# Output weights of a decode attention kernel: rows of 1 KB by head, in place of rows of 4 and 2 KB with selection matmuls

## The chip, the cores and the metric

The kernel runs on one core of a Trainium2 chip. The metric is the device time of one execution in microseconds. Three runs of the kernel before took 1382.37, 1382.78 and 1384.41 us; the median, 1382.78 us, is the time before.

## What is computed

Two attention blocks for one decoded token and four batches, each with its own query weights, caches and output weights; the outputs stand side by side. Block A has 32 query heads on 8 key heads and looks at the last 2048 positions; block B has 32 heads of its own and looks at all 8192. Everything is bfloat16, a head has 128 elements.

```python
# A: x (4,1,512), k/v cache (4,8,8192,128), W = 2048, rep = 4
q = (x @ wq) as (B, 32, 1, 128)
k, v = last W rows of the caches, each head repeated rep times
p = softmax(q k^T * 128 ** -0.5)
a = (p v) as (B, 1, 32 * 128) @ wo          # wo: (4096, 512)
# B: the same with k/v cache (4,32,8192,128), all rows, rep = 1
out = concatenate([a, b], axis=-1)
```

The caches that are read hold 570 MB, and each element is used for one or four query heads only, so nearly all of the work is to bring them in.

## The kernel before, in words

**Stages.** Stage A has 8 chunks, one for each key head with its four batches: 2 MB of keys and 2 MB of values. Stage B has 64 chunks, one for each pair of heads and each batch: 4 MB of keys and 4 MB of values. Chunk numbers run through: `NCA` = 8 is the first chunk of B, `NC` = 72 their number. A chunk is split into groups of 8 tiles of 128 x 128.

**One chunk.** PE transposes each key tile into PSUM (`tr`, `emit_T`), DVE or ACT copies a group to `kt` (L476, L474), PE multiplies it with the queries (`sc`, `emit_S`). DVE takes maxima (L539; in stage A first L523 and L525, which pick the scores of each partition's own batch), ACT takes the exponentials (`pba` in A, `pbb` in B). Two `ms` matmuls (`stats_gmax`, `stats_exp`) carry the maxima across partitions. Then PE multiplies the probabilities with the value tiles into `po` (`emit_pv`), `norm_sum` sums the rows with a matmul of ones and `norm_out` writes the normalised head outputs to `oT` (A: 4 heads x 4 batches) or `oz` (B: 2 heads x 4 batches, once in two chunks), with the 128 elements of a head on the partitions.

**Output weights.** The output product adds, for each head, a matmul of 128 x 4 with 128 x 512 to `fin`, in PSUM from the first chunk to the last (`emit_fin`). The weights come in per chunk of A (`wor`, 512 KB for 4 heads) and per head pair of B (`wos`, 256 KB). In the kernel before, partition p of `wor` takes the four consecutive rows 4p to 4p + 3 of the 512, so a row of the load is 4 KB long; partition p of `wos` takes rows 2p and 2p + 1, 2 KB. A partition then no longer holds element p of every head, but elements 4i + r (2i + r) of the head that its quarter (half) stands for. So the head outputs are permuted alike: `emit_sel` multiplies `oT` with four masks `sel4`, or `oz` with two masks `sel2`, into columns of `ms`, and DVE copies each quarter or half to `zA` or `zB` (L670). For the last pair it is turned about: `emit_wol` brings the weights back into head order with the masks `back2` (PE, four matmuls into `tr`) and copies them to `wol` (ACT and DVE, L682, L684), so that after the last `po` only `oz`, two `fin` matmuls, a copy and the output's DMA are left. POOL makes the masks at the start.

**Order.** Every engine has its program written out by hand: `sch.add` puts an instruction at the end of its engine's list, with the events that it waits for. `keys_part(c)` interleaves the transposes and scores of chunk c with pieces of earlier chunks at given groups: in A the maxima of chunk c - 1 at group 2 and its exponentials at 3, `emit_sel(c - 2)` at 4, `norm_sum(c - 1)` at 6 and `emit_fin(c - 2)` at 7; in B `emit_sel` at 8 and `emit_fin` at 10 of every second chunk. `values_part` has the value matmuls of the chunk before, and the last two groups of scores.

**Loads.** All large loads are issued by SP in one fixed order. In A it goes: keys of c + 1, values of c, `wor` of c, keys of c + 2, and so on. Keys wait until the buffer's earlier keys are transposed (L354), values until the earlier values are multiplied, `wor` of c until `fin` of c - 2 (L331). In B the order is keys, values, keys, values (L372), with one `wos` load ahead of every fourth keys (L338), which waits for the last `fin` that used it. The last keys come in two halves (L369, L370) and the last values in five pieces (L363).

Of the kernel before, what the change touches and what calls it, by code (L numbers as in the profile page):

```python
# [12 lines left out]
P = 128  # L13
# [6 lines left out]
NSM = 2  # L20
# [2 lines left out]
LASTV = (64, 32, 16, 8, 8)  # L23

TRM0, BC0, L0, Q0, XT0 = 0, 256, 288, 320, 448
Z0 = Q0


class _Record:
# [129 lines left out]
def bass_concat_heads__sliding_block_cached__mha_block_cached__decode_kernel(  # L159
# [45 lines left out]
    with ExitStack() as es:  # L205
        block = es.enter_context(nc.Block())

        def sb(name, shape, dt):
            return es.enter_context(nc.sbuf_tensor(name, shape, dt))
# [29 lines left out]
        oT = sb("oT", [P, NSM, 16], BF16)  # L239
        oz = sb("oz", [P, 8], BF16)  # L240
        outsb = sb("outsb", [36, DO], BF16)
        sel4 = sb("sel4", [P, 4, P], BF16)
        sel2 = sb("sel2", [P, 2, P], BF16)
        back2 = sb("back2", [P, 2, 2, P], BF16)
        zA = sb("zA", [P, 2, 16], BF16)
        zB = sb("zB", [P, 8], BF16)
        wol = sb("wol", [P, 2, DO], BF16)
        tr = ps("tr", [P, NTRB, TG * P], BF16)
        sc = ps("sc", [P, 2, 512], F32)
        po = ps("po", [P, 512], F32)  # L250
# [30 lines left out]
        sch.add("pool", lambda e: e.memset(pbt[1][:, :, :], 0.0), key=("c_pb", 1))  # L281

        for r in range(4):
            sch.add("pool", lambda e, r=r: e.affine_select(
                out=sel4[:, r, :], in_=onesb[:, :], pattern=[[0, 4], [-4, 32]], compare_op=ALU.is_equal,
                fill=0.0, base=-r, channel_multiplier=1), waits=["c_onesb"])
        for r in range(2):
            sch.add("pool", lambda e, r=r: e.affine_select(  # L290
                out=sel2[:, r, :], in_=onesb[:, :], pattern=[[0, 2], [-2, 64]], compare_op=ALU.is_equal,
                fill=0.0, base=-r, channel_multiplier=1))
            for u in range(2):
                sch.add("pool", lambda e, r=r, u=u: e.affine_select(
                    out=back2[:, u, r, :], in_=onesb[:, :], pattern=[[1, P]], compare_op=ALU.is_equal,
                    fill=0.0, base=P * u - r, channel_multiplier=-2), key="c_sel" if r == u == 1 else None)


        half_of = {}
        held = [[] for _ in range(NH)]  # L300
        HALF_A = {"k": (8, 9), "v": (4, 5)}
# [21 lines left out]
        def wo_slot(g):  # L323
            return g % 2 if g < NCA - 1 else 2

        def dma_wo(g):

            src = A_wo[g * 4 * P:(g + 1) * 4 * P, :].rearrange("(p r) n -> p (r n)", r=4)
            slot = wo_slot(g)
            dst = wor[:, slot, :]  # L330
            sch.add_dma("sp", lambda e: e.dma_start(dst, src), "d_wo%d" % slot,  # L331
                        waits=[("fin", g - 2)] if g >= 2 and slot < 2 else [], key=("wo", g))

        def dma_wos(hp):


            src = B_wo[2 * hp * P:2 * (hp + 1) * P, :].rearrange("(p r) n -> p (r n)", r=2)
            sch.add_dma("sp", lambda e: e.dma_start(wos[:, :, :].rearrange("p r n -> p (r n)"), src), "d_wos",  # L338
                        waits=[("fin", NCA + 4 * hp - 1)] if hp else [], key=("wos", hp))

        def dma_kv(kind, c):
# [302 lines left out]
        def norm_out(c):  # L644
            if 0 <= c < NCA:
                m = c % NSM
                o, i0, i1 = oT[:, m, :], po[:, m * 16:m * 16 + 16], rinv[:, m, :]
            else:

                o, i0 = oz[:, :].rearrange("p (x y) -> p x y", x=2), bcast(po[:, 0:4], [[0, 2], [1, 4]])  # L650
                i1 = rz[:, :].rearrange("p (x y) -> p x y", x=2)
            waits = [("rinv" if 0 <= c < NCA else "rz", c), ("pv", c)] + ([("sm", c - 2 if c != NCA + 1 else NONE)] if c >= 2 else [])
            sch.add("dve", lambda e: e.tensor_tensor(out=o, in0=i0, in1=i1, op=ALU.mult), waits=waits, key=("oT", c))
            po_read[:] = [("oT", c)]

        def emit_sel(c):

            if 0 <= c < NCA:
                sel, x, n, z, k = sel4, oT[:, c % NSM, :], 16, zA[:, c % 2, :], 4
                free = [("fin", c - 2)] if c >= 2 else []  # L660
            else:
                sel, x, n, z, k = sel2, oz[:, :], 8, zB[:, :], 2
                free = [("fin", c - 2 if c - 2 >= NCA else NONE)] if c != NONE else []
            for r in range(k):
                pe_mm(ms[:, Z0 + r * n:Z0 + (r + 1) * n], sel[:, r, :], x,
                      waits=[("oT", c)] + ms_read if r == 0 else [], key=("sm", c) if r == k - 1 else None)
            for h in range(k):
                pp = slice(h * P // k, (h + 1) * P // k)
                src = ms[pp, Z0:Z0 + k * n].rearrange("p (r b h) -> p h r b", r=k, b=NB)[:, h]
                sch.add("dve", lambda e, src=src, pp=pp: e.tensor_copy(z[pp, :].rearrange("p (r b) -> p r b", r=k), src),  # L670
                        waits=[("sm", c)] + free if h == 0 else [], key=("z", c) if h == k - 1 else None)
            ms_read[:] = [("z", c)]

        def emit_wol():

            for u in range(2):
                o = tr[:, u, :].bitcast(F32)
                for r in range(2):
                    pe_mm(o, back2[:, u, r, :], wos[:, r, :], start=r == 0, stop=r == 1,
                          waits=[("wos2", NC - 1)] if u == r == 0 else [], key=("back", u) if r else None)  # L680
                if u == 0:
                    sch.add("act", lambda e, o=o: e.activation(wol[:, 0, :], o, ACTF.Copy), waits=[("back", 0)], key=("wol", 0))  # L682
                else:
                    sch.add("dve", lambda e, o=o: e.tensor_copy(wol[:, 1, :], o), waits=[("back", 1)], key=("wol", 1))  # L684

        def emit_fin(c):
            ab = 0 if 0 <= c < NCA else 1
            p0 = 0 if ab == 1 else 32
            if c == NC - 1:
                ov = oz[:, :].rearrange("p (b u) -> p b u", u=2)  # L690
                ops = [(ov[:, :, u], wol[:, u, :]) for u in range(2)]
                waits = [("oT", c), ("wol", 0), ("wol", 1)]
            elif ab == 1:
                ops = [(zB[:, r * NB:(r + 1) * NB], wos[:, r, :]) for r in range(2)]
                waits = [("z", c), ("wos2", c)]
            else:
                w = wor[:, wo_slot(c), :].rearrange("p (r n) -> p r n", r=4)
                ops = [(zA[:, c % 2, r * NB:(r + 1) * NB], w[:, r, :]) for r in range(4)]
                waits = [("z", c), ("wo", c)]
            lastc = NC - 1 if ab == 1 else NCA - 1  # L700
            for i, (l, r) in enumerate(ops):
                pe_mm(fin[p0:p0 + NB, :], l, r, start=False, stop=i == len(ops) - 1 and c == lastc,
                      waits=waits if i == 0 else [], key=("fin", c) if i == len(ops) - 1 else None)
            if c == lastc:
                sch.add("dve", lambda e: e.tensor_copy(outsb[p0:p0 + NB, :], fin[p0:p0 + NB, :]), waits=[("fin", c)], key=("osb", ab))
                sch.add_dma("sp" if ab == 1 else "act",
                            lambda e: e.dma_start(out[:, 0, ab * DO:(ab + 1) * DO], outsb[p0:p0 + NB, :]),
                            "d_o%d" % ab, waits=[("osb", ab)], key=("out", ab))
# [6 lines left out]
        def keys_part(c):  # L715
# [3 lines left out]
            for g in range(ch["NG"]):  # L719
# [8 lines left out]
                if 1 <= c < NCA and g == 6:  # L728
                    norm_sum(c - 1)
                if 2 <= c < NCA and g == 4:  # L730
                    emit_sel(c - 2)
                if 2 <= c < NCA and g == 7:
                    emit_fin(c - 2)
                if c >= NCA and c % 2 == 0 and g == 6:
                    norm_sum(ahead(c, 1))
                if c >= NCA and c % 2 == 1 and g == 8:
                    emit_sel(ahead(c, 2))
                if c >= NCA and c % 2 == 1 and g == 10:
                    emit_fin(ahead(c, 2))

# [25 lines left out]

        def finish_A():
            stats_gmax(NCA - 1)
            emit_sel(NCA - 2)
            stats_exp(NCA - 1)  # L770
            emit_fin(NCA - 2)
            norm_sum(NCA - 1)
            for g in range(chunks[NCA - 1]["NG"]):
                emit_pv(NCA - 1, g)
            pv_done(NCA - 1)
            emit_sel(NCA - 1)
            emit_fin(NCA - 1)

        emit_xT()
# [2 lines left out]
        for c in range(NC):  # L782
            if c == NCA:
                sch.mark()
                finish_A()
            keys_part(c)
            if c == 0:
                emit_q(1)

                pe_mm(fin[0:36, :], pbt[0][:, 1, 0:36], pbt[0][:, 1, 0:DO], stop=False, waits=["c_sel"])  # L790
            values_part(None if c == 0 else NONE if c == NCA else c - 1, c)
        sch.mark()
        norm_sum(NC - 1)
        emit_wol()
        for g in range(chunks[NC - 1]["NG"]):
            emit_pv(NC - 1, g)
        pv_done(NC - 1)
# [60 lines left out]
```

## Time and profile before

| | |
|---|---|
| median of three runs | 1382.78 us |
| profiled execution: time / span | 1382.37 / 1380.6 us |
| PE, DVE, ACT, POOL busy | 85%, 48%, 32%, 1% of the span |
| DMA, main queue | 587.22 MB, 25208 packets, 99.4% of 16 engines' span |
| keys of B, 4 MB | 26.8 us from issue to landing |
| `wor`, 512 KB (8 loads) / `wos`, 256 KB (16 loads) | 6.0 / 20.4 us from issue to landing |
| L670 to `zA` (32) / to `zB` (64) | 168 / 164 ns each on DVE |

The span is one execution by the hardware profiler; the time adds what lies around it. Every load is cut into packets (one for each contiguous row, shared among 16 DMA engines), and the profile counts them and the share of time in which the engines had one. "L408" is a line of the kernel's file; all matmuls are recorded at L408 and all transposes at L406, so they are told apart by the tile that they write. "x24" is a count.

### The profile page before, as it was taken

To read this page: it belongs to the slowest core of one execution; us is meant where nothing else is said; L and a number is where in the kernel's file an instruction comes from. 1 tells how busy PE (TensorE), PEld (TensorE's weight loads), DVE (VectorE), ACT (ScalarE), POOL (GpSimd) and SP (SyncE) were. 2 spreads that over 40 slices of the span, in tenths; PEclk is the share of its full clock that TensorE was granted. 3 is DMA by queue.
4 is the path that set the end of the run, shared out by engine and by line. 5 is a ranking of instruction groups with operands and counts; after the bars stand their busy time and mean duration, and the time that the engine had idled before them with its cause. 6 is when DMAs were issued, how large, how long until landed. Compare 5 with 4: busy or idle time off the path is not lost.

```text
span 1380.6 us, 59798 instructions
## 1 busy us (share of the span) xinstructions
PE 1175.7 (85%) x27001; PEld 1131.6 (82%) x27001; DVE 656.8 (48%) x1434; ACT 436.7 (32%) x650; POOL 7.4 (1%) x28
## 2 busy tenths in 40 slices
PE   4887898888889888888898888888988898888988
PEld 4776898887888888888898888787987888888887
DVE  1665464444445444444454445444544444444444
ACT  1543233332233323322333223232332233223332
POOL 2000000000000000000000000000000000000000
PEclk9899999999999999999999999999999999999999
DMA  9999999999999999999999999999999999999998
GB/s 401 421 393 402 388 439 426 432 433 428 438 430 428 433 428 438 430 429 433 428 431 436 429 433 428 431 436 432 430 432 427 436 432 430 433 426 432 437 425 349
DMA packets 25254, 587.53 MB, mean 426 GB/s; under 512 B 2817, under 2 KB 2833, under 8 KB 6289
## 3 DMA queue, kind: packets, MB, share of 16 engines
q1 hardware_dynamic: 25208, 587.22, 99.4%
q8 instruction: 16, 0.26, 0.1%
q14 instruction: 6, 0.04, 0.0%
q10 hardware_dynamic: 24, 0.01, 0.0%
HBM read 587.21 MB, written 0.01 MB: 425 GB/s over the span
## 4 chain that ended last, share of the span: by engine, by line
DMA 60%; PE 35%; DVE 3%; issue 1%; ACT 1%; DVEq 0%; SPq 0%; ACTq 0%
DMA kv<-in_B_k_cache_dram 56%; PE tr L406 21%; PE sc L408 9%; PE po L408 3%; DMA kv<-in_B_v_cache_dram 2%; DMA kv<-in_B_wq_dram 2%; PE fin L408 2%; PE ms L408 1%; DVE sA L525 1%; DVE kt L476 0%; DVE zA L670 0%; DVE sA L523 0%; ACT pba L588 0%; DVE sA L581 0%; ACT eA L585 0%
## 5 line engine op out<-in xcount | busy, mean ns | idle before, releaser
L406 PE MATMUL tr<-identb,kv 128*128 128x128 bf16 x8704 | 697.2, 230 | 160.0 <-DMA kv<-in_B_k_cache_dram 156.9
L476 DVE COPY kt<-tr 128x1024 bf16<-128x1024 bf16 x736 | 502.5, 691 | 441.5 <-PE tr L406 436.8
L406 PEld LDWEIGHTS tr<-identb,kv 128*128 128x128 bf16 x8704 | 552.7, 104 | 182.0 <-DMA kv<-in_B_k_cache_dram 98.3
L474 ACT ACTIVATE kt<-tr 128x1024 bf16<-128x1024 bf16 x352 | 360.3, 1024 | 629.3 <-PE tr L406 629.3
L408 PE MATMUL sc<-qb,kt 128*128 128x64 bf16 x8704 | 448.9, 196 | 11.6 <-DVE kt L476 11.4
L408 PEld LDWEIGHTS sc<-qb,kt 128*128 128x128 bf16 x8704 | 370.1, 101 | 16.9 <-DVE kt L476 13.8
L408 PE MATMUL po<-pbb,kv 128*128 128x64 bf16 x8320 | 293.9, 192 | 6.3 <-issue 4.4
L408 PEld LDWEIGHTS po<-pbb,kv 128*128 128x128 bf16 x8320 | 267.1, 97 | 8.6 <-issue 4.6
L573 ACT ACTIVATE pbb<-sc,negb 64x128 bf16<-64x128 f32 x128 | 51.2, 400 | 294.9 <-DVE negb L563 294.1
L539 DVE TENSOR_REDUCE rm<-sc 64x1 f32<-64x128 f32 x128 | 36.9, 289 | 95.1 <-PE sc L408 94.2
L551 DVE TENSOR_REDUCE gm<-ms 1x2 f32<-1x128 f32 (+1 forms) x72 | 20.1, 279 | 44.8 <-PE ms L406 44.7
L563 DVE COPY negb<-ms 128x1 f32<-128x1 f32 (+1 forms) x72 | 11.4, 159 | 53.6 <-PE ms L408 53.6
L408 PE MATMUL ms<-identf,gx 1*128 1x1 f32 (+1 forms) x144 | 27.6, 259 | 0.8 <-DVE zA L670 0.8
L408 PEld LDWEIGHTS ms<-identf,gx 1*128 1x128 f32 (+1 forms) x144 | 21.5, 186 | 4.9 <-DVE zA L670 0.9
L573 ACT ACTIVATION_READ_ACCUMULATOR pbb<-sc,negb 64x1 f32 x128 | 23.7, 185 | 0.0
L406 PE MATMUL ms<-identf,rm 128*1 128x128 f32 (+1 forms) x72 | 19.6, 273 | 2.3 <-DVE rm L534 2.3
L408 PE MATMUL po<-pba,kv 128*128 128x64 bf16 x512 | 19.8, 198 | 0.5 <-ACT pba L588 0.5
L408 PEld LDWEIGHTS po<-pba,kv 128*128 128x128 bf16 x512 | 17.5, 101 | 3.2 <-issue 2.6
L408 PE MATMUL fin<-wos,zB 128*4 128x512 bf16 x64 | 19.0, 378 | 0.0
L555 DVE TENSOR_SCALAR gx<-gm 1x128 f32<-1x128 f32 (+1 forms) x72 | 15.9, 221 | 2.5
L523 DVE TENSOR_SCALAR sA<-sc,mk 128x256 f32<-128x256 f32 x8 | 3.9, 484 | 23.2 <-PE sc L408 23.2
L408 PE MATMUL ms<-xT,kv 128*128 128x4 bf16 x256 | 7.1, 166 | 8.9 <-DMA kv<-in_A_wq_dram 4.5
(61 smaller groups left out, 175.5 us busy)
## 6 DMA issues: line engine op xcount, KB each, us to landing
kv<-in_B_k_cache_dram SPq DMA_DIRECT2D x63, 4096.0 KB, 26.8
kv<-in_B_v_cache_dram SPq DMA_DIRECT2D x63, 4096.0 KB, 31.6
kv<-in_A_k_cache_dram SPq DMA_DIRECT2D x8, 2048.0 KB, 11.5
kv<-in_A_v_cache_dram SPq DMA_DIRECT2D x8, 2048.0 KB, 13.3
kv<-in_A_wq_dram SPq DMA_DIRECT2D x1, 4096.0 KB, 12.3
kv<-in_B_wq_dram SPq DMA_DIRECT2D x1, 4096.0 KB, 27.3
wor<-in_A_wo_dram SPq DMA_DIRECT2D x8, 512.0 KB, 6.0
wos<-in_B_wo_dram SPq DMA_DIRECT2D x16, 256.0 KB, 20.4
```

Of the source, the lines that this page charges most:

```text
L406: sch.add("pe", lambda e: e.transpose(o, l, r), waits, key)
L408: sch.add("pe", lambda e: e.matmul(o, l, r, start=start, stop=stop), waits, key)
L474: sch.add("act", lambda e: e.activation(dst, src, ACTF.Copy), waits=waits, key=("ev", s))
L476: sch.add("dve", lambda e: e.tensor_copy(dst, src), waits=waits, key=("ev", s))
L523: emit = lambda e, src=src: e.tensor_scalar(out=t, in0=src, scalar1=mk[:, 0:1], scalar2=None, op0=ALU.mult)
L525: emit = lambda e, src=src, b=b: e.scalar_tensor_tensor(out=t, in0=src, scalar=mk[:, b:b + 1], in1=t, op0=ALU.mult, op1=ALU.add)
L539: sch.add("dve", lambda e, src=src, pp=pp: e.tensor_reduce(out=rm[pp, m, 0:1], in_=src, axis=AX.X, op=ALU.max), waits=[("S", ch["s_last"]) ...
L551: sch.add("dve", lambda e: e.tensor_reduce(out=gm[0:C, m, 0:U], in_=src, axis=AX.X, op=ALU.max), waits=[("trm", c)], key=("gmax", c))
L555: sch.add("dve", lambda e: e.tensor_scalar(out=dst, in0=gv, scalar1=-scale, scalar2=None, op0=ALU.mult), waits=[("gmax", c)], key=("gx", c))
L563: sch.add("dve", lambda e: e.tensor_copy(negb[:, m, 0:C], ms[:, col:col + C]), waits=[("bc", c)], key=("negb", c))
L573: sch.add("act", lambda e, src=src, pp=pp, n=n, u=u: e.activation(pbv[pp, :, u], src, ACTF.Exp, bias=negb[pp, m, 0:1], scale=scale, accum_ ...
```

## The change

The rows of the output weights are loaded by head: partition d takes row d of each of the 4 (2) heads, so that each load has 4 (2) rows of 1 KB per partition. The masks, `emit_sel`, `emit_wol`, `zA`, `zB` and `wol` go, and `emit_fin` takes its 128 x 4 operands from `oT` and `oz` directly. `emit_fin(c - 2)` stands in A at group 4, where the selection was, and no longer at 7; in B it stays at group 10. `norm_out` waits for `fin` of two chunks before where it waited for the selection. The bytes loaded and SP's order of loads are the same.

```diff
         def dma_wo(g):
-            src = A_wo[g * 4 * P:(g + 1) * 4 * P, :].rearrange("(p r) n -> p (r n)", r=4)
+            src = A_wo[g * 4 * P:(g + 1) * 4 * P, :].rearrange("(hl d) n -> d hl n", d=P)
             slot = wo_slot(g)
-            dst = wor[:, slot, :]
+            dst = wor[:, slot, :].rearrange("p (hl n) -> p hl n", hl=4)
...
         def dma_wos(hp):
-            src = B_wo[2 * hp * P:2 * (hp + 1) * P, :].rearrange("(p r) n -> p (r n)", r=2)
-            sch.add_dma("sp", lambda e: e.dma_start(wos[:, :, :].rearrange("p r n -> p (r n)"), src), "d_wos",
+            src = B_wo[2 * hp * P:2 * (hp + 1) * P, :].rearrange("(hl d) n -> d hl n", d=P)
+            sch.add_dma("sp", lambda e: e.dma_start(wos[:, :, :], src), "d_wos",
...
-            waits = [...] + ([("sm", c - 2 if c != NCA + 1 else NONE)] if c >= 2 else [])
+            waits = [...] + ([("fin", c - 2 if c != NCA + 1 else NONE)] if c >= 2 else [])
...
-        def emit_sel(c):
-            for r in range(k):
-                pe_mm(ms[:, Z0 + r * n:Z0 + (r + 1) * n], sel[:, r, :], x, ...)
-            for h in range(k):
-                sch.add("dve", lambda e: e.tensor_copy(z[pp, :]..., src), ...)
-        def emit_wol():
...
         def emit_fin(c):
-            if c == NC - 1:
+            if ab == 1:
                 ov = oz[:, :].rearrange("p (b u) -> p b u", u=2)
-                ops = [(ov[:, :, u], wol[:, u, :]) for u in range(2)]
-                waits = [("oT", c), ("wol", 0), ("wol", 1)]
-            elif ab == 1:
-                ops = [(zB[:, r * NB:(r + 1) * NB], wos[:, r, :]) for r in range(2)]
-                waits = [("z", c), ("wos2", c)]
+                ops = [(ov[:, :, u], wos[:, u, :]) for u in range(2)]
+                waits = [("oT", c), ("wos2", c)]
             else:
-                ops = [(zA[:, c % 2, r * NB:(r + 1) * NB], w[:, r, :]) for r in range(4)]
-                waits = [("z", c), ("wo", c)]
+                ov = oT[:, c % NSM, :].rearrange("p (u c) -> p u c", c=REP)
+                ops = [(ov[:, :, cc], w[:, cc, :]) for cc in range(REP)]
+                waits = [("oT", c), ("wo", c)]
...
                 if 2 <= c < NCA and g == 4:
-                    emit_sel(c - 2)
-                if 2 <= c < NCA and g == 7:
                     emit_fin(c - 2)
...
-                if c >= NCA and c % 2 == 1 and g == 8:
-                    emit_sel(ahead(c, 2))
                 if c >= NCA and c % 2 == 1 and g == 10:
                     emit_fin(ahead(c, 2))
...
         norm_sum(NC - 1)
-        emit_wol()
         for g in range(chunks[NC - 1]["NG"]):
             emit_pv(NC - 1, g)
```

More of the change, by code (lines that the diff above doesn't have):

```diff
@@ L25 @@
 TRM0, BC0, L0, Q0, XT0 = 0, 256, 288, 320, 448
-Z0 = Q0
 class _Record:
@@ L241, in bass_concat_heads__sliding_block_cached__mha_block_cached__decode_kernel @@
         outsb = sb("outsb", [36, DO], BF16)
[L242 to L247, printed above, removed]
         tr = ps("tr", [P, NTRB, TG * P], BF16)
@@ L281, in bass_concat_heads__sliding_block_cached__mha_block_cached__decode_kernel @@
         sch.add("pool", lambda e: e.memset(pbt[1][:, :, :], 0.0), key=("c_pb", 1))
[L285 to L296, printed above, removed]
         half_of = {}
@@ L651, in norm_out @@
                 i1 = rz[:, :].rearrange("p (x y) -> p x y", x=2)
-            waits = [("rinv" if 0 <= c < NCA else "rz", c), ("pv", c)] + ([("sm", c - 2 if c != NCA + 1 else NONE)] if c >= 2 else [])
+            waits = [("rinv" if 0 <= c < NCA else "rz", c), ("pv", c)] + ([("fin", c - 2 if c != NCA + 1 else NONE)] if c >= 2 else [])
             sch.add("dve", lambda e: e.tensor_tensor(out=o, in0=i0, in1=i1, op=ALU.mult), waits=waits, key=("oT", c))
             po_read[:] = [("oT", c)]
-        def emit_sel(c):
[L658 to L663, printed above, removed]
-            for r in range(k):
-                pe_mm(ms[:, Z0 + r * n:Z0 + (r + 1) * n], sel[:, r, :], x,
-                      waits=[("oT", c)] + ms_read if r == 0 else [], key=("sm", c) if r == k - 1 else None)
-            for h in range(k):
[L668 to L672, printed above, removed]
-        def emit_wol():
[L676 to L684, printed above, removed]
         def emit_fin(c):
@@ L688, in emit_fin @@
             p0 = 0 if ab == 1 else 32
-            if c == NC - 1:
+            if ab == 1:
                 ov = oz[:, :].rearrange("p (b u) -> p b u", u=2)
-                ops = [(ov[:, :, u], wol[:, u, :]) for u in range(2)]
-                waits = [("oT", c), ("wol", 0), ("wol", 1)]
-            elif ab == 1:
-                ops = [(zB[:, r * NB:(r + 1) * NB], wos[:, r, :]) for r in range(2)]
-                waits = [("z", c), ("wos2", c)]
-            else:
-                w = wor[:, wo_slot(c), :].rearrange("p (r n) -> p r n", r=4)
-                ops = [(zA[:, c % 2, r * NB:(r + 1) * NB], w[:, r, :]) for r in range(4)]
-                waits = [("z", c), ("wo", c)]
+                ops = [(ov[:, :, u], wos[:, u, :]) for u in range(2)]
+                waits = [("oT", c), ("wos2", c)]
+            else:
+                w = wor[:, wo_slot(c), :].rearrange("p (hl n) -> p hl n", hl=4)
+                ov = oT[:, c % NSM, :].rearrange("p (u c) -> p u c", c=REP)
+                ops = [(ov[:, :, cc], w[:, cc, :]) for cc in range(REP)]
+                waits = [("oT", c), ("wo", c)]
             lastc = NC - 1 if ab == 1 else NCA - 1
@@ L768, in finish_A @@
             stats_gmax(NCA - 1)
-            emit_sel(NCA - 2)
+            emit_fin(NCA - 2)
             stats_exp(NCA - 1)
-            emit_fin(NCA - 2)
             norm_sum(NCA - 1)
@@ L775, in finish_A @@
             pv_done(NCA - 1)
-            emit_sel(NCA - 1)
             emit_fin(NCA - 1)
@@ L788, in bass_concat_heads__sliding_block_cached__mha_block_cached__decode_kernel @@
                 emit_q(1)
-                pe_mm(fin[0:36, :], pbt[0][:, 1, 0:36], pbt[0][:, 1, 0:DO], stop=False, waits=["c_sel"])
+                pe_mm(fin[0:36, :], pbt[0][:, 1, 0:36], pbt[0][:, 1, 0:DO], stop=False, waits=[("c_pb", 1)])
             values_part(None if c == 0 else NONE if c == NCA else c - 1, c)
```

## The prediction

> **What bounds the kernel now.** I read the page first, then the chain that ended last, then the stages by windows, then SP's and the engines' order in time around the changed lines, then the tail.
>
> ```profile
> DMA  9999999999999999999999999999999999999998
> q1 hardware_dynamic: 25208, 587.22, 99.4%
> ```
>
> The DMA engines are busy in every slice; PE's 85% is not the limit. What a load costs is engine time per row, so I took the packet records of the trace (start, duration and size of every packet): a 32 KB packet takes 1216 ns (median), 16 KB 611, 8 KB 313, 4 KB 159, 2 KB 84, and the 4 B packet that closes a load on each engine 9. That is about 37.7 ns per KB and 8.5 ns per packet, whatever its size. The chain shows what a row load does to the clock:
>
> ```profile
> 702.67 26.81 DMA kv<-in_B_k_cache_dram
> ...
> 743.24 25.09 DMA kv<-in_B_k_cache_dram
> ...
> 781.05 26.84 DMA kv<-in_B_k_cache_dram
> ```
>
> A line with DMA is start and length up to landing. Key chunks land at 702.67 + 26.81 = 729.48, then 768.33, then 807.89 us. Two chunks of keys and values lie between; the first gap is 38.85 us, the second 39.56. The second holds one `wos` load (its packets run from 795.4 to 797.6), so that load costs 0.71 us. By packets it is 8 per engine x 84 + 9 = 681 ns. In stage B an extra packet is paid in full.
>
> ```profile
> 1.00:82.00 81.00, 56.35 (x1136) 50.90 (x1137) 34.32 (x92) 29.75 (x41) 6.96 (x24) 0.89 0.99 413
> 82.00:111.00 29.00, 23.39 (x509) 20.25 (x505) 18.05 (x52) 13.23 (x19) 0.00 (x0) 1.00 0.90 359
> ```
>
> Of the windows, the last two columns are DMA share and GB/s. Stage A lives on a backlog until 82 us; from there to 111 the DMA engines have 29 x 0.10 = 2.9 us of nothing to do. The holes are where SP comes late:
>
> ```profile
> 81.77 0.33 SPq L331 DMA_DIRECT2D wor<-in_A_wo_dram  x1
> 82.15 0.54 SPq L354 DMA_DIRECT2D kv<-in_A_k_cache_dram  x1
> ...
> 93.98 0.33 SPq L331 DMA_DIRECT2D wor<-in_A_wo_dram  x1
> ```
> ```profile
> SPq L331 <- PE fin L408: 46.8, 5, 9.8
> PE tr L406 <- DMA kv<-in_B_k_cache_dram: 156.9, 58, 4.4
> ```
>
> SP holds a key load behind a `wor` load that waits for `fin`; a head's cycle is 93.98 - 81.77 = 12.2 us, set by PE with DVE. In stage B PE waits 156.9 / 58 = 2.7 us for most key chunks: that is cover there.
>
> **The change part by part.** All sums are against the profiled execution: 1382.37 us, of which the span is 1380.6. The median of the runs is 1382.78, so I add the sum to that.
>
> *B's rows.* Each of the 16 `wos` loads goes from 8 rows of 2 KB per engine to 16 of 1 KB. The trace has few packets of 1 KB: the x loads at 45 ns and the output at 48 to 49, with the engines nearly idle; the line through the other sizes gives 37.7 + 8.5 = 46.3. So 16 x 46.3 + 9 = 750 in place of 681 ns: +0.069 us, x16 = **+1.10 us**. Bounds: 42 ns (half the 2 KB packet, nothing paid per row) gives 0; 84 ns (a 1 KB row as dear as 2 KB) gives 8 x 84 x 16 = +10.8 us. I take 46.3, because the 1 KB packets themselves stand beside it and the per-packet part is the same from 2 KB to 16 KB under load.
>
> *A's rows.* Each of the 8 `wor` loads goes from 8 rows of 4 KB to 32 of 1 KB: 32 x 46.3 - 8 x 159 = +0.21 us, x8 = **+1.68 us** of engine time; by the same bounds +0.6 and +11.3.
>
> The Trainium skill, "DMA: Bandwidth & Descriptors", section "Why small descriptors are slow (HBM only)", speaks against the change with a smaller price: about 3 cycles per packet beside one per 32 B, so 35 for a 1 KB row, 67 for 2 KB, 131 for 4 KB. By it (an estimate: 70/67 and 140/131 of the packets above) the two parts are +0.5 and +0.7 us, and the whole sum would be -2.4 us. Its section "Specifications" has 512 B as enough for line rate, by which the rows cost nothing; the 84 ns of 2 KB, against 76 at the rate of 32 KB, already says otherwise.
>
> *A's order.* What goes, per head from the third on, and what moves:
>
> ```profile
> 89.41 0.25 PE L408 MATMUL ms<-oT,sel 128*128 128x16 bf16 x4
> ...
> 91.08 0.71 DVE L670 CAST zA<-ms 32x16 bf16<-32x16 f32 x4
> ...
> 91.85 0.39 PE L408 MATMUL ms<-rsa,onesf 128*128 128x16 f32 x2 [0.22 <-DVE zA L670]
> ...
> 92.93 1.02 PE L408 MATMUL fin<-wor,zA 128*4 128x512 bf16 x4
> ```
>
> Four selections (0.11 us of PE's sequence, T(5) starts at 89.49 instead of 89.38) and four casts (0.71 us of DVE, which hold the row-sum matmul 0.22 us and the next `kt` copy from 91.17 to 91.83) go. The four `fin` matmuls of 0.95 us move from behind T(7) to where the selection stood. There PE has 0.44 us of waiting for a `kt` copy at 91.22 to give them, and the scores of group 5 wait for ACT's copy until 92.53 in any case. So `po` can follow at about 92.95 instead of 93.9: a cycle of some 11.3 us in place of 12.2. SP gains more: `wor` is issued some 3.5 us earlier in the cycle, and the key load behind it when the transposes are done (about 92.6) and not after `fin` (93.98). DMA needs, per head, 16 packets of 16 KB and 32 of 1 KB: 16 x 0.611 + 1.48 = 11.3 us. Both sides balance, with the backlog of the start still there, so I expect the 2.9 us of holes to be filled: **-2.9 us**. If PE's cycle did not shorten at all, the longer `wor` loads up to 106 us (7 x 0.21 = 1.5) would still run in those holes: -1.5 is the other end. A gain beyond 2.9 is excluded: no engine can be more than busy. The value of the upper end is taken because the key loads alone move by 1.4 us per head.
>
> *Queues.* Behind the longer `wor` on SP stand the next keys. In the tail five issues in a row took 9.65 us (L363), the last of them 7.0: SP stalls when some 80 rows per engine are queued. The second `wor`, at 26 us, would meet that and hold SP to about 36; the next issue is due at 44.14. Nothing is late. In stage B 53 rows stand where 45 stood.
>
> *B's selections* (2 matmuls, 2 casts per pair, 0.2 us PE and 0.34 us DVE) go beside PE's 2.7 us waits for keys: 0. If that cover were gone, 32 x 0.2 = 6 us at most would be gained, but it cannot go while DMA sets the pace. The ten masks on POOL (about 3 us in the first 9) precede the query weights' landing at 13 us: 0.
>
> *The tail.* The un-permuting of the last weights stands on the chain:
>
> ```profile
> 1372.59 0.88 PE tr L408 x4
> 1373.47 3.76 PE po L408 x128
> ```
>
> Without it `po` starts 0.88 us earlier. Its last 8 tiles would come at 1372.59 + 120 x 0.0294 = 1376.12, but the slowest engine lands the last values at 1376.28 (landing records): **-0.7 us**; 0 and -0.88 are the ends. What is late next is that landing.
>
> Sum: 1.10 + 1.68 - 2.9 - 0.7 = -0.8 us: **1382.0 us**. A difference under 0.2% (2.8 us) is about what a measurement of this kernel cannot tell from no change; this one is far below.
>
> **The rivals.**
> *Short rows cost more under load (slower).* 512 rows of 1 KB per engine (16 x 16 + 8 x 32) multiply every error: each ns over 46.3 is 0.51 us. At 60 ns the sum is -0.8 + 512 x 0.0137 = +6.2: 1389.0 us. It decides from 46.3 + 3.6 / 0.512 = 53 ns on. For it: no loaded 1 KB packet is in the trace, and 4 KB packets of four `wor` loads that ran at the holes average 184 to 214 ns. Against: 2 KB under full load keeps 84 to 85 in all 16 loads.
> *Rows are nearly free (faster).* At 42 ns: 0 + 0.6 - 2.9 - 0.7 = -3.0: 1379.8 us, just over the bound. Against it is the 8.5 ns seen at every size.
> *The holes stay (no change).* The engines of stage A do not speed up: 2.78 - 1.5 - 0.7 = +0.6: 1383.4 us. For it: PE and DVE have little idle time there.
>
> **How the numbers follow.** The forecast has 0.45 and the holes that stay 0.15; both are within 0.2%, 0.60 together. Dearer rows 0.28, free rows 0.12. The range is 1379.6 to 1389.0: below lies some 0.06 of the free rows, above some 0.12 of the dear ones.
>
> **What would show it.** Right: 1 KB packets of 45 to 48 ns; a `wos` load that parts two key landings by 39.63 and not 39.56 us; DMA share 0.97 or more between 82 us and the end of stage A; a head's cycle near 11.3 us; no `tr` piece before the last `po`. Wrong: 1 KB packets above 53 ns in stage B, holes of DMA still there before the first B keys, new ones when A hands over to B (131 to 157 us, where two loads were issued just in time), or a last `po` that waits for values by more than 0.3 us.

## The result, and the profile after

The changed kernel takes 1378.29 us (median of 6 runs, 1377.69 to 1381.14) against 1383.68 us of the kernel before (6 runs, 1382.37 to 1386.97): a ratio of 0.9963, with a 95% interval of 0.9948 to 0.9978. That is 5.1 us faster (3.0 to 7.2). The forecast was 1382.0 us in a range that began at 1379.6, and a gain above 0.2% had a chance of 0.12. It was too pessimistic.

One thing has to be known before two profiles are laid side by side. The profiled execution of before that the prediction read (1382.37 us) was the shortest of that kernel's runs; the first one of after (1380.55 us, span 1378.8) is one of the longer of its runs. The two spans differ by only 1.8 us. I therefore took both kernels again: `before_again` (span 1383.5) and `after_again` (span 1376.7), which stand close to the medians. Where it matters I show those.

The page of after, its slices of DMA time and its main queue:

```profile
DMA  9999999999999999999999999999999999999998
q1 hardware_dynamic: 30328, 587.22, 99.7%
```

5120 packets more than before, as the rows of 1 KB ask for, and yet a share of 99.7% where it was 99.4%. The windows that the prediction looked at (busy time of PE, weight loads, DVE, ACT and POOL, the granted clock, DMA share, GB/s), first of after, then of `after_again`:

```profile
82.00:111.00 29.00, 23.99 (x460) 20.51 (x458) 18.66 (x48) 14.43 (x21) 0.00 (x0) 0.93 1.00 405
```
```profile
82.00:111.00 29.00, 25.58 (x524) 21.97 (x525) 18.26 (x47) 17.11 (x26) 0.00 (x0) 1.00 1.02 416
```

The share was 0.90 at 359 GB/s. The holes of stage A are closed. A share of 1.02 is no slip: the records of packets overlap, so that at times more than 16 packets are under way on the 16 engines, and the share counts them all.

The chain of waits shows key landings in stage B of after:

```profile
778.65 27.30 DMA kv<-in_B_k_cache_dram
...
818.62 26.18 DMA kv<-in_B_k_cache_dram
...
857.14 27.27 DMA kv<-in_B_k_cache_dram
```

They land at 805.95, 844.80 and 884.41: 38.85 us without a `wos` load between, 39.61 with one. Before it was 38.85 and 39.56, and 39.63 was forecast.

SP's queue in stage A of `after_again`:

```profile
74.46 0.37 SPq L308 DMA_DIRECT2D wor<-in_A_wo_dram  x1
76.59 0.54 SPq L330 DMA_DIRECT2D kv<-in_A_k_cache_dram  x1
...
85.63 0.37 SPq L308 DMA_DIRECT2D wor<-in_A_wo_dram  x1
87.75 0.54 SPq L330 DMA_DIRECT2D kv<-in_A_k_cache_dram  x1
...
96.85 0.37 SPq L308 DMA_DIRECT2D wor<-in_A_wo_dram  x1
```

A head's cycle is 85.63 - 74.46 = 11.2 us, where it was 12.2 (11.3 was forecast), and the key load no longer goes out together with `wor` but 2.1 us behind it, when the transposes are done. And PE, in the same cycle:

```profile
84.57 1.03 PE L384 MATMUL fin<-wor,oT 128*4 128x512 bf16 x4
...
85.98 0.37 PE L384 MATMUL sc<-qb,kt 128*128 128x64 bf16 x8
...
87.66 0.41 PE L384 MATMUL sc<-qb,kt 128*128 128x64 bf16 x8
```

No line here ends in a bracket: PE waits for no `kt` copy between `fin` and `po`. The end of the chain of after:

```profile
1342.06 32.88 DMA kv<-in_B_v_cache_dram
...
1374.99 0.43 PE po L384 x8
...
1375.73 0.61 PE fin L384 x2
...
1376.36 0.68 DVE outsb L649
```

No `tr` piece is left before the last `po`, and what sets the end now is the landing of the last values at 1374.94 us, which the prediction named as what is late next; PE waits 0.22 us for it.

### The profile page after: what moved, and what is told of

It reads as the page before. It is cut to its first block, busy times and chain, and to the rows that moved or that the text cites. A ratio compares the mean times of both kernels' runs of the same rounds, so it can differ in the third digit from the quotient of the medians.

```text
span 1378.8 us, 59410 instructions
## 1 busy us (share of the span) xinstructions
PE 1179.3 (86%) x26901; PEld 1134.8 (82%) x26901; DVE 641.3 (47%) x1337; ACT 436.0 (32%) x649; POOL 4.8 (0%) x18
## 3 DMA queue, kind: packets, MB, share of 16 engines
q1 hardware_dynamic: 30328, 587.22, 99.7%
## 4 chain that ended last, share of the span: by engine, by line
DMA 58%; PE 37%; DVE 2%; issue 1%; SPq 1%; ACT 0%; DVEq 0%
DMA kv<-in_B_k_cache_dram 54%; PE tr L382 22%; PE sc L384 10%; PE po L384 3%; DMA kv<-in_B_v_cache_dram 2%; PE fin L384 2%; DMA kv<-in_B_wq_dram 2%; DVE sA L501 1%; PE ms L384 1%; SPq L339 1%; DVE kt L452 0%; DVE sA L499 0%; ACT pba L564 0%; PE ms L382 0%; DVE rm L510 0%
## 5 line engine op out<-in xcount | busy, mean ns | idle before, releaser
L382 PEld LDWEIGHTS tr<-identb,kv 128*128 128x128 bf16 x8704 | 559.4, 105 | 181.2 <-DMA kv<-in_B_k_cache_dram 97.0
L384 PEld LDWEIGHTS sc<-qb,kt 128*128 128x128 bf16 x8704 | 369.7, 100 | 13.8 <-DVE kt L452 11.1
L384 PE MATMUL fin<-wos,oz 128*4 128x512 bf16 x66 | 19.6, 378 | 0.3 <-DVE oz L629 0.3
L384 PEld LDWEIGHTS ms<-xT,kv 128*128 128x128 bf16 x256 | 7.0, 104 | 9.3 <-DMA kv<-in_A_wq_dram 4.7
## 6 DMA issues: line engine op xcount, KB each, us to landing
kv<-in_B_k_cache_dram SPq DMA_DIRECT2D x63, 4096.0 KB, 27.3
kv<-in_A_k_cache_dram SPq DMA_DIRECT2D x8, 2048.0 KB, 12.6
kv<-in_A_v_cache_dram SPq DMA_DIRECT2D x8, 2048.0 KB, 14.2
kv<-in_A_wq_dram SPq DMA_DIRECT2D x1, 4096.0 KB, 12.2
```

Of the source, the lines that this page charges most:

```text
L382: sch.add("pe", lambda e: e.transpose(o, l, r), waits, key)
L384: sch.add("pe", lambda e: e.matmul(o, l, r, start=start, stop=stop), waits, key)
```

## The ledger

So every item that was to be seen was seen, and the time still was nearly 4 us lower than forecast. The packet records (start, duration and size of every packet) say where it is. A hole is counted here wherever fewer than 16 packets are under way, an overlap wherever more are; both are divided by 16, as the time of the packets is. In us, of the two profiles close to the medians (differences are taken before rounding):

| | before_again | after_again | difference |
|---|---|---|---|
| packets of 1, 2 and 4 KB (mostly output weights) | 24.7 | 27.3 | +2.6 |
| packets of 16 and 32 KB (nearly all keys and values) | 1344.2 | 1342.5 | -1.7 |
| all other packets | 5.2 | 5.3 | +0.1 |
| overlap, to be taken off | 5.5 | 6.8 | -1.4 |
| holes, start to 200 us | 7.2 | 2.5 | -4.7 |
| holes, 1350 us to the end | 7.6 | 5.8 | -1.8 |
| sum, and the span | 1383.5 | 1376.7 | -6.9 |

In the row of the holes to 200 us, 2.1 us on each side are the kernel's start. From 200 to 1350 us no profile here has any. The last row but one is mostly an accident of these two executions: in `before_again` PE's granted clock is 0.5 from 1367.6 to 1371.0 us. From the end of the last 32 KB packet to the end of the span it takes 16.1 us, but 14.7 in `before`, `keys_first` and `a_only`, which have the same tail and no such stretch of clock there. With the new tail it is 14.2 to 14.3.

The holes by stretch, all kernels (those of the experiments are explained below), the time at which PE starts to transpose the first keys of B, and the time at which SP issues B's third keys, which wait for these transposes:

| profile | holes 60-130 us | holes 130-200 us | first transposes of B | third keys of B issued |
|---|---|---|---|---|
| before | 3.2 | 1.3 | 134.0 | 144.8 |
| before_again | 1.5 | 3.6 | 134.2 | 145.3 |
| rows_only | 2.6 | 3.4 | 133.7 | 144.8 |
| keys_first | 4.9 | 1.6 | 135.0 | 146.5 |
| tail_only | 1.7 | 3.6 | 133.9 | 145.4 |
| fin_late | 2.6 | 1.2 | 132.4 | 143.3 |
| after | 0.6 | 1.6 | 131.3 | 142.2 |
| after_again | 0.0 | 0.5 | 125.9 | 136.7 |
| order_only | 0.0 | 0.5 | 126.3 | 137.2 |
| mixed | 0.0 | 0.4 | 126.4 | 137.3 |
| a_only | 0.0 | 1.4 | 130.0 | 140.8 |
| late_handover | 0.0 | 6.2 | 133.3 | 146.2 |

The prediction counted 2.9 us up to 111 us and none after it. The profiles with PE's order of before in stage A (the first five rows) have 4.5 to 6.5 us in the two stretches together, those with the changed order (`after` to `a_only`) 0.4 to 2.1, and part of both lies where A hands over to B. How the holes are shared between the stretches changes from one execution of a kernel to the next. Their sum follows the last column: the time of the third keys less the sum of the holes is 138.8 to 140.3 us in all rows but three, and in these three there are hardly any holes. So the holes of A and those behind it belong together: whether they fall into A or behind it, there are fewer of them when PE lets the third keys go out earlier.

## Experiments

Each kernel was timed beside the kernel before on the same chip, five rounds, unless it says otherwise. Changes in us are worked out from the ratio, whose 95% interval stands beside it.

**The parts by themselves: rows, order.** `rows_only` is the kernel before with the loads of both weights written as rows of 1 KB to the same places, selection and order untouched:

```diff
-            src = A_wo[...].rearrange("(p r) n -> p (r n)", r=4)
-            dst = wor[:, slot, :]
+            src = A_wo[...].rearrange("(p r) n -> p r n", r=4)
+            dst = wor[:, slot, :].rearrange("p (r n) -> p r n", r=4)
```
(and the same for `wos` with r=2)

> The kernel before with its selection, masks and order kept; only the loads of the output weights are cut into 1 KB rows (same places in the buffers, same output). Theory 1 (every packet is paid, as the prediction has it): +2.8 us of packets less what the idle DMA time of stage A takes up, +1.3 to +2.8 us against the kernel before. Theory 2 (short rows are nearly free, the gain is all from the order): 0 to +1 us, the 16 loads of stage B showing +0.04 to +0.07 us each. Theory 3 (long rows are what was dear, short ones gain by themselves): -2 us or more.

Measured: 1385.06 us against 1385.08; 1.0001 (0.9992 to 1.0009), 0 +- 1.2 us. But its main queue shows that the rows did not become shorter:

```profile
q1 hardware_dynamic: 25208, 587.22, 99.1%
```

25208 packets are those of the kernel before (30328 in after), with the same 1152 of 4 KB and 2304 of 2 KB. The four (two) rows of 1 KB lie behind one another on both sides of this load, and they went as one packet, as before. So none of the three theories is tested: this is the kernel before once more, and shows how well two sets of its runs agree. What 1 KB rows cost in the order of before, no run here shows.

`order_only` is the changed kernel with the loads of before, in rows of 4 and 2 KB (25208 packets); the heads then meet other rows of the weights, and the work is the same:

```diff
-            src = A_wo[...].rearrange("(hl d) n -> d hl n", d=P)
+            src = A_wo[...].rearrange("(p r) n -> p (r n)", r=4)
```
(and the same for `wos` with r=2)

> The changed kernel, with no selection and with fin at group 4, but with the weights loaded in 4 and 2 KB rows as before; the heads then meet the wrong rows of the weights, the work is the same. Theory 1: the full order gain without the packets: 2.8 us faster than the changed kernel, -3.6 us against before by the predicted sum, about -8 us if the measured -5.4 us has the packets in it. Theory 2: as the changed kernel within 1 us, -4 to -6 us against before. Theory 3: -2 to -3 us, slower than the changed kernel.

Measured: 1376.98 us against 1385.08; 0.9946 (0.9933 to 0.9958), so -7.5 us (5.8 to 9.3).

`after_again`, the changed kernel in the same comparison:

> The changed kernel, unaltered, for a second profile and more times. All theories: -4 to -6 us against the kernel before. If the 1.4 us of idle DMA at 163.5 to 166 us in the first profile is an accident of PE's clock, it is shorter or absent when the execution is one of the shorter ones (1378 us); if it belongs to the change, it is there again.

Measured: 1379.75 us; 0.9964 (0.9951 to 0.9977), -5.0 us. The hole at 163.5 to 166 us is absent. `before_again`, one profiled execution of the kernel before:

> The kernel before, unaltered, for a second profile. The idle DMA time of stage A (0.6 us at 82, 0.25 at 94.5, 2.0 at 106 to 111) and of the start of stage B (0.3 at 146 to 158, 1.0 at 166 to 169) is there again if it belongs to the kernel; what moves by more than 1 us between the two profiles is scatter of one execution.

Measured: 1385.37 us. The holes of the two stretches are 1.5 and 3.6 us where the first profile had 3.2 and 1.3: their places are scatter by more than 1 us, their sum (5.1 and 4.5) is not.

What follows: in the new order 1 KB rows cost some 2.5 us (0.9964 against 0.9946), near the sum's +2.78. The two intervals overlap a little, so the packets have to say it too: from `order_only` to `after_again` those of 1, 2 and 4 KB rise from 23.9 to 27.3 us, of which 1.3 come back by overlap, 2.2 us net. What was mis-sized is the gain of order and tail together, -3.6 in the sum and -7.5 measured.

**What made the cycle shorter: the queue or PE?** The prediction gave two causes for the holes: a key load held on SP behind a `wor` load that waits for `fin`, and PE's and DVE's cycle. The expectations call the first theory S and the second P, with P1 for the place of `fin` on PE. `keys_first` takes away the first cause alone: in the kernel before, SP issues `wor` behind the next keys.

```diff
+        late_wo = []
...
-                dma_wo(c)
+                late_wo.append(c)
+            if (kind == "k" and c < NCA) or (kind == "v" and c == NCA - 1):
+                while late_wo:
+                    dma_wo(late_wo.pop(0))
```

> The kernel before, with one change on SP: in stage A each wor load is issued behind the next keys and not ahead of them, so that no key load waits for fin. Theory S (the holes in the loads of stage A come from keys held behind wor on SP): the keys are issued about 1.4 us earlier, the holes at 82 and 94 us close, -1 to -2.5 us. Theory P (the holes are what is left when the head's cycle of PE and DVE, 12.2 us, is longer than the 11.1 us of its loads): the cycle stays at 12.2 us, the holes move but do not go, within 1 us of the kernel before.

Measured: 1384.19 us against 1384.06; 1.0008 (0.9999 to 1.0017). No gain. SP's queue of `keys_first`:

```profile
79.89 0.54 SPq L354 DMA_DIRECT2D kv<-in_A_k_cache_dram  x1
81.13 0.33 SPq L331 DMA_DIRECT2D wor<-in_A_wo_dram  x1
...
92.09 0.54 SPq L354 DMA_DIRECT2D kv<-in_A_k_cache_dram  x1
```

The keys now go first and 1.24 us ahead of `wor`, but the cycle is 92.09 - 79.89 = 12.2 us as before, and the holes are no smaller. When a load goes out within the cycle is worth nothing here as long as the cycle stays.

`fin_late` is the changed kernel with `fin` back at group 7; selections and casts stay away:

```diff
-                if 2 <= c < NCA and g == 4:
+                if 2 <= c < NCA and g == 7:
                     emit_fin(c - 2)
```

> The changed kernel with fin of stage A back at group 7; no selection, rows of 1 KB. Theory P1 (the place of fin makes the cycle short, its matmuls fill PE's wait for a copy): the cycle is 11.9 to 12.2 us, most of the order gain of stage A is lost, 3 to 5 us slower than the changed kernel. Theory P2 (the casts and selections that went make it short): the cycle stays below 11.6 us, within 1.5 us of the changed kernel. Theory S: wor and keys are late as before, the cycle is short, holes in the loads of stage A of 1 us or more.

Measured: 1382.22 us against 1384.06; 0.9988 (0.9978 to 0.9997), -1.7 us. Some 3.5 us of the gain are gone, and the cycle is 12.2 us again. PE in the timeline of `fin_late`:

```profile
91.02 0.41 PE L384 MATMUL sc<-qb,kt 128*128 128x64 bf16 x8 [0.54 <-DVE kt L452]
...
92.39 0.41 PE L384 MATMUL sc<-qb,kt 128*128 128x64 bf16 x8 [0.30 <-ACT kt L450]
...
92.73 1.03 PE L384 MATMUL fin<-wor,oT 128*4 128x512 bf16 x4
```

The brackets are PE's waits for the copies of `kt`: 0.84 us, which are back, and `fin` comes after them. At group 4 its 0.95 us lie in these waits, which the lines of `after_again` above don't have. So the place of `fin` on PE makes the cycle, and not the casts that went from DVE nor the order on SP.

**The tail.** `tail_only` is the kernel before with the last pair's weights loaded by head and without `emit_wol`. In it, and in `mixed` below, the heads of the last pair's first batches meet these weight rows in another order; the work is the same.

```diff
...
+            if hp == HB // 2 - 1:
+                src = B_wo[...].rearrange("(hl d) n -> d hl n", d=P)
+                dst = wos[:, :, :]
...
-                ops = [(ov[:, :, u], wol[:, u, :]) for u in range(2)]
+                ops = [(ov[:, :, u], wos[:, u, :]) for u in range(2)]
...
-        emit_wol()
```

> The kernel before with the weights of the last head pair alone loaded by head in 1 KB rows, so that the un-permuting in the tail (four matmuls, two copies) goes; all else is as before. The prediction's term: -0.7 us. If PE's half clock in the tail, seen in the second profile of the kernel before, belongs to the matmuls that went, or if the whole tail is paid on PE's chain: -0.9 to -2.5 us. If the tail is set by the last landing already: 0.

Measured: 1383.99 us against 1384.06; 0.9996 (0.9987 to 1.0005), so -0.6 +- 1.2 us. This can't tell the -0.7 of the sum from nothing. The profiles say a little more: 14.7 us from the last 32 KB packet to the end with the old tail and 14.2 to 14.3 with the new, where the clock is full in both, so -0.5 us.

**Stage A alone, with and without the tail.** `a_only` has the changed stage A (rows, order, no selection) and all of B as before:

```diff
-            src = A_wo[...].rearrange("(p r) n -> p (r n)", r=4)
+            src = A_wo[...].rearrange("(hl d) n -> d hl n", d=P)
...
-                ops = [(zA[:, c % 2, r * NB:(r + 1) * NB], w[:, r, :]) for r in range(4)]
+                ops = [(ov[:, :, cc], w[:, cc, :]) for cc in range(REP)]
...
-                    emit_sel(c - 2)
-                if 2 <= c < NCA and g == 7:
                     emit_fin(c - 2)
...
             stats_gmax(NCA - 1)
-            emit_sel(NCA - 2)
+            emit_fin(NCA - 2)
             stats_exp(NCA - 1)
-            emit_fin(NCA - 2)
...
-            emit_sel(NCA - 1)
             emit_fin(NCA - 1)
```

The last lines are the end of A (`finish_A`), where the last two heads are finished before PE turns to B; the changed kernel has them too.

> Stage A as in the changed kernel (1 KB rows, no selection, fin at group 4); stage B and the tail wholly as before (2 KB rows, selection, un-permuting in the tail). If the whole gain is stage A's: -5 to -7 us against the kernel before, and 0 to 1.5 us faster than the changed kernel, since the rows of stage B stay at 2 KB. If stage B's part of the change brings a gain of its own (the tail, or no selection at the start of the stage): slower than the changed kernel.

Measured: 1378.31 us against 1384.01; 0.9959 (0.9945 to 0.9973), -5.7 us. `mixed` adds the edit of `tail_only` to it:

> Stage A as in the changed kernel (1 KB rows, no selection, fin at group 4), stage B as before (2 KB rows, two selection matmuls and two casts per pair) but for the last pair, which is loaded by head. Theory 1 (in stage B each row is paid, the selection is hidden there): 15 loads x 0.05 to 0.07 us = 0.75 to 1.0 us faster than the changed kernel. If the selection in stage B costs something at the start of the stage, where PE sets when loads are issued: as the changed kernel or slower. Against the kernel before: -5 to -7 us.

Measured: 1377.43 us against 1384.06; 0.9952 (0.9939 to 0.9966), -6.6 us. All of the gain that these times can resolve is stage A's, its end included; `a_only` can't be told from the changed kernel. `mixed` pays for 1 KB rows in A and in one load of B only. It lies 0.9 us below the changed kernel by medians, but the intervals overlap, so it is not shown to be better; as it stands it gives a time only, since two batches of the last pair meet the wrong rows.

**Is the rest at the hand-over?** If the gain beyond the holes of stage A comes from PE reaching B earlier, then holding PE there, and nowhere else, must give it back. `late_handover` is the changed kernel with 24 idle matmuls of 512 columns at the start of the end of stage A, behind the last head's scores:

```diff
+            for _ in range(24):
+                pe_mm(tr[:, 0, :].bitcast(F32), identb[:, :], kt[:, 0, 0:512])
```

> The changed kernel with 24 idle matmuls of 512 columns put on PE where stage A ends (some 5 to 6 us), so that stage B starts about as late against its first loads as before; the head's cycle and the loads of stage A are untouched. Theory H (a good part of the gain is that PE comes early enough to stage B for its first value and key loads): the holes between 130 and 200 us come back to 1.5 us or more, +1.5 to +3 us against the changed kernel. If all of the gain is made in the holes of stage A before 111 us: within 0.7 us of the changed kernel.

Measured: 1384.05 us against 1384.01; 1.0003 (0.9994 to 1.0012). The gain is gone entirely, some 5.5 us (1.0003 against 0.9963 and 0.9964 of the changed kernel) where theory H expected 1.5 to 3, though the cycle in stage A stays at 11.1 to 11.3 us and the engines have no holes there. PE between A and B, of `before_again`, `after_again` and `late_handover`:

```profile
132.39 1.87 PE L408 MATMUL fin<-wor,zA 128*4 128x512 bf16 x4 [0.81 <-DVE zA L670]
134.19 2.07 PE L406 MATMUL tr<-identb,kv 128*128 128x128 bf16 x24
```
```profile
124.57 1.35 PE L384 MATMUL fin<-wor,oT 128*4 128x512 bf16 x4 [0.34 <-DVE oT L629]
125.86 1.51 PE L382 MATMUL tr<-identb,kv 128*128 128x128 bf16 x24
```
```profile
112.68 5.34 PE L384 MATMUL tr<-kt,identb 128*128 128x512 bf16 x24
...
126.23 1.82 PE L384 MATMUL fin<-wor,oT 128*4 128x512 bf16 x4 [0.34 <-DVE oT L629]
133.31 2.74 PE L382 MATMUL tr<-identb,kv 128*128 128x128 bf16 x24 [5.26 <-issue]
```

The idle matmuls lie partly in waits that PE has there in any case, so `fin` ends only 2.1 us later than in `after_again`; the other 5.26 us are "issue", a wait for nothing that the profile shows. Together B's first transposes come at 133.3 us in place of 125.9. Behind them stand the loads: the buffer of B's third keys is free when PE has transposed the first, and SP issues that load at 136.69 us in `after_again`, 145.34 in `before_again` and 146.16 in `late_handover`. What the engines make of it, in the windows of the same three:

```profile
130.00:150.00 20.00, 18.28 (x398) 16.47 (x396) 10.29 (x23) 5.12 (x5) 0.00 (x0) 0.87 0.96 398
150.00:175.00 25.00, 21.05 (x437) 20.04 (x433) 10.31 (x23) 6.94 (x13) 0.00 (x0) 0.86 0.89 359
```
```profile
130.00:150.00 20.00, 15.59 (x354) 15.32 (x352) 7.94 (x19) 5.38 (x9) 0.00 (x0) 0.91 1.00 429
150.00:175.00 25.00, 20.95 (x440) 20.08 (x437) 10.31 (x19) 6.94 (x11) 0.00 (x0) 0.86 1.00 422
```
```profile
130.00:150.00 20.00, 16.68 (x369) 16.68 (x370) 8.77 (x17) 5.12 (x5) 0.00 (x0) 0.83 0.79 325
150.00:175.00 25.00, 17.56 (x383) 16.63 (x380) 9.18 (x19) 6.03 (x9) 0.00 (x0) 0.93 0.92 381
```

0.96 and 0.89, 1.00 and 1.00, 0.79 and 0.92: by packet records the holes from 130 to 200 us are 3.6, 0.5 and 6.2 us. With no holes in A and third keys as late as before, all the holes of before, and 1.1 us more, stand behind A. So closing the holes of A would have been worth little if PE had not come to B earlier.

## Why the prediction was wrong, step by step

**The step that failed: "A's order, -2.9".** The way from the edit to PE's cycle was right: a cycle of 11.2 us where 11.3 was forecast, `fin` in PE's wait for a `kt` copy, and the holes before 111 us that close. Wrong was the sentence "A gain beyond 2.9 is excluded: no engine can be more than busy". It took the holes of one window for all the holes there are: 4.5 to 6.5 us with the old order, 0.4 to 2.1 with the new. Up to the last head's scores PE gains 7.0 us (`before_again` against `after_again`), and the end of A is 1.3 us shorter without selections and casts: 8.3 us together at B's first transposes, 134.2 to 125.9. The prediction followed that only as far as the last loads of A. Its next step would have been to ask who waits for PE at the start of B: the keys of two chunks are loaded ahead, and the third keys wait for the transposes of the first. The trace of before had a hint, the hole at 166.8 to 168.8 us that I had not looked for; the prediction even named 131 to 157 us as the place where loads were issued just in time, but only as a danger. `late_handover` shows that a delay of PE there alone costs as much as the whole change gains, and `order_only` that order and tail give 7.5 us where 3.6 stood.

Wrong too was one of the two causes given for the holes, the key load that SP holds behind `wor`: `keys_first` takes it away and gains nothing. That the key loads move by 1.4 us per head was no reason for the upper end.

Not all of the miss is holes. From `before_again` to `order_only`, whose profiled execution was a short one, the span falls by 10.1 us: 4.7 are holes up to 200 us, 2.3 holes in the tail (mostly the clock, as said above), and 3.1 shorter times of packets of the same sizes, which the sum had taken as fixed. Why these are shorter is not shown.

**Part of the miss is the profile that was read.** The first profile of before had 4.5 us of holes after 60 us; `before_again` and `rows_only`, the same work, have 5.1 and 6.0. A sum "against its own time" was added to a median, but the holes of the shortest execution are not those of the median.

**The rows, +2.78: about right.** Rows of 1 KB take 46 ns (median, mean 46.7) in stage B and 49.2 on average in stage A under full load, where 46.3 was taken. Against `order_only` the packets cost 3.5 us more, of which 1.3 come back because records overlap; some 2.5 us were measured. The estimate from the Trainium skill ("DMA: Bandwidth & Descriptors", "Why small descriptors are slow (HBM only)"), +1.2 us for both parts, is below the 2.2 us net of the packets and the 2.5 measured, and the 512 B for line rate of its "Specifications", by which rows cost nothing, holds in no packet here: 46.7 ns per KB against 38.1 in a 32 KB packet (1219 / 32). That A's longer loads "would still run in those holes" if the cycle stayed long is not tested, since `rows_only` kept the long rows.

**The tail, -0.7: not resolved by times.** In the profiles with a full clock in the tail it is -0.5 us, 14.7 to 14.2 or 14.3; in `tail_only` -0.6 +- 1.2.

**Queues, B's selections, POOL's masks, 0 each: nothing speaks against it.** `a_only` keeps B's selections and can't be told from the changed kernel.

**The rivals.** The dearer rows are refuted by the packets (46 ns, not 60), the free rows by the same packets (46 ns, not 42), with which `order_only` agrees, and the holes that stay by the windows. None of them had the mechanism that decided; a rival on the faster side had only been sought among row costs, not among the holes.

**Open.** Why PE waits up to 5.3 us for "issue" at the start of B was not tried. So how much of `late_handover`'s loss belongs to the idle matmuls and how much to the wait that they brought with them is not separated; the hole itself is measured either way.

## What to carry to other kernels

Where DMA sets the pace, count every hole of the DMA engines from the packet records, from the first load to the last, and ask of an engine's saved time what it releases in the next stage, not only in its own. Here 1 us per head on PE paid because it brought forward the first load of B that waits for PE; the holes of A by themselves were not the measure. Before a sum is made against one profile, see where its time stands among the kernel's runs. And before an experiment on a load is read, see by its packet count that the load did change.

## What I had not expected of the hardware

- DMA shares above 1: 1.02 to 1.03 in stage A with 1 KB rows. The packet records overlap more there, 6.8 us in `after_again` against 5.5 in `order_only`.
- Rows that lie behind one another on both sides of a load went as one packet, though the load was written as rows of 1 KB: 25208 packets in `rows_only` as in the kernel before.
- Packets of one size differ in their mean though not in their median: 4 KB rows take 173 to 177 ns on average in the two profiles of before, 161.6 in `order_only` (159 in the median of each), 16 KB packets of the loads 623 to 626 and 616 ns. It is not the holes alone: `keys_first` has the most of them and 160.4 ns for 4 KB rows. There the keys, not `wor`, are the first load behind a hole.
- PE's "issue" waits at the start of B, in the first code behind A's heads: 1.97, 2.45 and 3.18 us in `after_again`. A packet of 16 KB of the instruction queue, about 1.1 us long, lies among the loads near each of them, and the wait ends 1.4 to 1.5 us after that packet; the 5.26 us in `late_handover` end 1.7 us after one. That PE waits for its instructions there is argued from that, not shown.
- The runs of one kernel differ by 2 to 6 us. Half-clock windows of PE of 3.4 us fall into stage A in some executions and not in others: a granted clock of 0.93 in after and of 1.00 in `after_again` in the windows above. Where one falls into a cycle of `after` it takes 12.6 us and not 11.2, and the hand-over comes later (131.3 against 125.9 us).
